# Hourglass attention and a MoE layer: both heads of a pair side by side in batch 0's AV output, transposed and up-sampled together

## Chip, cores, metric

One core of a Trainium2 chip. The metric is the device time of one execution in microseconds (us), the median of several runs. Engines: TensorE (PE, its weight loads PEld), VectorE (DVE), ScalarE (ACT), GpSimd (POOL), SyncE (SP).

## What is computed

Two layers, one after the other. The attention has two branches: one in which each query sees the keys within three positions, and one over sequences that are averaged by four, whose result is repeated four times. Their sum, tokens by 512, goes through a layer with a gated activation.

```python
# q, k, v: (8 batches, 8 heads, 576 tokens, 64)
q_d = q.reshape(B, H, Sd, 4, D).mean(axis=3)        # k_d, v_d alike; Sd = 144
out_up = np.repeat(sm_attn(q_d, k_d, v_d), 4, axis=2)
mask = np.abs(pos[:, None] - pos[None, :]) < 4      # local branch
scores = np.where(mask, scale * np.matmul(q, kT), -1e9)
attn_out = out_up + np.matmul(softmax(scores), v)
x = attn_out.transpose(0, 2, 1, 3).reshape(4608, 512)
h = x @ w_in                                        # (512, 2048)
out = (h / (1 + exp(-1.702 * h))) @ w_out           # (2048, 512)
```

## The kernel before

Heads go in four pairs (`hp`), with 64 values a head, so that a pair fills 128 partitions. The result of the attention is kept transposed, in `xT[hp]`, 128 partitions by all tokens; the MoE layer reads it in 9 groups of 512 tokens (`mm1`: 16 column blocks of `w_in`, four matmuls each, a silu on ScalarE; `mm2`: 4 token blocks, 16 matmuls each against `w_out`). Group 0 needs only batch 0. The attention of batch g + 1 is laid as `steps` between the matmuls of group g (L881-887), so batch 0 alone stands before any matmul that could cover it. The order on every engine is the order in which the code issues (`manual_schedule`, L44); POOL and SP also issue the DMAs, in that order.

The local branch works on 5 chunks of 114 queries, each as two halves (`par`) of 60 queries against 64 keys. The steps of batch 0:

- Scores, exponentials, and the cast of v into `vb` by VectorE, chunk by chunk as it lands (L777).
- `av_local` (L434): per chunk, half and head (`j`) a 64x64 matmul into one bank for each `par`; a head is put into partitions 0 to 63 or 64 to 127 by `pos`. Column 64 of each 65 is the sum of the weights. `warm` (L605) is a fp32 matmul of 512 columns on zeros that nobody reads; three of them stand between the parts (L795, L798).
- `prep_vd_pe` (L337): sums of four tokens of v, as 14 matmuls with the 0/1 matrix `psel` into `PA[2]`, then one ScalarE copy of 768 columns into `vd` (L352).
- `av_down` (L448): the averaged branch, 20 matmuls a head pair. Three blocks of 48 of its 144 queries come out in two columns (slots 5 and 6) of two banks.
- `normalise` (L470): a reciprocal of 14 sums and one product over 896 elements into `y`, on VectorE, per head pair; pair 3 uses the two banks `PM`, one at a time.
- `transp_sum` (L512): multiplies the averaged output with `up`, a 0/1 matrix that repeats each column four times (8 matmuls of 285 or 114 columns and 4 of 3 columns), and adds the 20 transposed 60x64 blocks of the local output in the same banks, by matmuls with an identity. Each matmul gives 64 partitions, so each is issued once for each head.
- `copy_x` (L553): four copies to `xT`, on ScalarE; for pair 3 the half `par` = 1 on VectorE.

The tail (L794-838) orders this and the first 24 matmuls of group 0: `turned` is `transp_sum` with `copy_x`; `part` issues matmuls of six accumulators `acc`, which lie in `PA` (three tiles of two banks), as soon as their `xT` is there. From column block 6 on, `late` says which bank `mm1` uses.

For batch 1, VectorE's transposes of q and k follow in its queue behind the last `copy_x`. The load of v for batch 1 (SP) waits for a VectorE copy behind those (L853), and on POOL the loads of the third and fourth quarter of `w_out` wait for that v (L855-859).

Of the kernel before, what the change touches and what calls it, by code (L numbers as in the profile page):

```python
# [8 lines left out]
FP32 = mybir.dt.float32  # L9
# [10 lines left out]
def kernel(  # L20
# [61 lines left out]
    UP = 5 + 240  # L82
# [30 lines left out]
    def iota_up():  # L113
        for par in range(2):
            for c in (0, 192):
                n = min(UP - c, 192)
                nc.gpsimd.iota(du[halves[par], c : c + n], pattern=[[1, n]],
                               base=-5 - 96 * par - (192 if c else 0) + c,
                               channel_multiplier=-1, **it)
# [217 lines left out]
    def prep_vd_pe(b, p, hp0=0, n=HP):  # L337
        vb, vd = vbs[b % 2], vds[b % 2]
        pv = p.rearrange("p x n -> p (x n)")
        for kc, iis in ((0, (0, 1)), (1, (1, 2, 3)), (2, (3, 4))):  # L340
            for i in iis:
                for j in range(2):
                    nc.tensor.matmul(  # L343
                        pv[64 * j : 64 * j + 64, 256 * kc : 256 * kc + D * n],
                        lhsT=psel[:, PSEL.index((i, kc)), :],
                        rhs=vb[:, i, :, :].rearrange(
                            "p (hp j) d -> p hp j d", j=2
                        )[:, hp0 : hp0 + n, j, 0:D],
                        start=(i == iis[0]), stop=(i == iis[-1]),
                        tile_position=(0, 64 * j),  # L350
                    )
        nc.scalar.copy(  # L352
            out=vd[:, :, hp0 : hp0 + n, 0:D],
            in_=pv[:, 0:768].rearrange("p (k h d) -> p k h d", k=3, h=HP)[:, :, 0:n],
        )
# [155 lines left out]

    def transp_sum(y, x):  # L512
        c0 = 20
        for par in range(2):
            edge = (0, 0) if par == 0 else (573, 285)
            for i0, ni, slot, t0 in ((0, 5, 5, 0), (2 - par, 2, 6, -192)):
                for j in range(2):
                    base = c0 + 384 * j + t0
                    nc.tensor.matmul(
                        sub(x[par][64 * j : 64 * j + 64], 57 * i0 + 3 * (1 - par),  # L520
                            (57, ni), (1, 57)),
                        lhsT=y[:, j, slot, :],
                        rhs=sub(up, base + 3 + 57 * par + 114 * i0, (114, ni), (1, 57)),
                        start=(slot == 5), stop=True,
                        tile_position=(0, 64 * j),
                        skip_group_check=True,
                    )
            for j in range(2):
                nc.tensor.matmul(
                    x[par][64 * j : 64 * j + 64, edge[1] : edge[1] + 3],  # L530
                    lhsT=y[:, j, 5, :],
                    rhs=sub(up, c0 + 384 * j + edge[0], (1, 3)),
                    start=False, stop=True,
                    tile_position=(0, 64 * j),
                    skip_group_check=True,
                )
        for i in range(5):
            for par in range(2):
                for j in range(2):
                    pos = j if par == 0 else 1 - j  # L540
                    c0 = 0 if (par == 1 or i == 0) else 3
                    c1 = 60 if (par == 0 or i == 4) else 57
                    nc.tensor.matmul(
                        x[par][64 * j : 64 * j + 64, 57 * i + c0 : 57 * i + c1],
                        lhsT=y[64 * pos : 64 * pos + 60, par, i, :],
                        rhs=ident(pos, 60, c0, c1),
                        start=False, stop=True,
                        tile_position=(64 * pos, 64 * j),
                        skip_group_check=True,
                    )  # L550
        return x

    def copy_x(b, hp, x):  # L553
        t0 = b * S
        for par in range(2):
            cp = nc.vector.tensor_copy if par and hp == HP - 1 else nc.scalar.copy
            cp(
                out=sub(xT[hp], t0 + 3 + 57 * par, (114, 5), (1, 57)),
                in_=sub(x[par], 3 - 3 * par, (57, 5), (1, 57)),
            )  # L560
            cp(
                out=sub(xT[hp], t0 + 573 * par, (1, 3)),
                in_=sub(x[par], 285 * par, (1, 3)),
            )
# [229 lines left out]
    for i0, i1 in ((0, 3), (3, 4)):  # L794
        warm(1)  # L795
        for hp in range(2):
            av_local(0, hp, o[hp], range(i0, i1))
    warm(1)  # L798
    prep_vd_pe(0, PA[2])
    make_mask()  # L800
    for hp in range(2):
        av_local(0, hp, o[hp], range(4, 5))
    for hp in range(2):
        av_down(0, hp, o[hp])
        y[hp] = normalise(o[hp])
    o[2] = av(0, 2, 2)
    y[2] = normalise(o[2])
    o[3] = PM
    av_local(0, 3, PM)
    av_down(0, 3, PM)  # L810
    y[3] = normalise(PM)

    gT0 = new_gT()
    acc = [PA[n][:, u, :] for n in range(3) for u in range(2)]
    late = PM + [acc[n] for n in (0, 2, 4)] + PM + [acc[1]] + PM
# [11 lines left out]
    turned(0, 0)  # L827
# [5 lines left out]
    turned(3, None)  # L833
# [84 lines left out]
```

## Time and profile before

| | us |
|---|---|
| median of 4 runs | 330.91 (329.95 to 332.26) |
| the profiled execution | 330.44 |
| its span, first to last instruction | 328.7 |
| TensorE busy in 0 to 19 us | 15.20 |
| TensorE busy in 19 to 31 us | 9.04 |
| TensorE busy in 31 to 43 us | 12.00 |
| TensorE busy in 43 to 66 us | 20.91 |
| TensorE busy in 66 to 180 us | 112.42 |
| TensorE busy in 180 to 328.7 us | 144.65 |

The granted TensorE clock is 1.00 in each of these stretches. The mean busy share of the DMA engines is 0.7 or more in every slice of the page up to 90 us.

How to read the lines that follow. A group line gives the source line, the engine, the operation, what is written and read, shapes (partitions x elements), the count, and then busy time, mean ns and idle time. A timeline line gives start, duration, engine, source line, operation, and in brackets the idle time of the engine just before and what ended it; "issue" means that nothing the profile shows ended it. A line of the waits gives total, number of times and longest, all in us. A line of the chain gives shares of the span.

### The profile page before, as it was taken

The page shows a single profiled execution, that of the slowest core. Times are in us where ns is not written, and L with a number is a line of the kernel's source. Part 1 is how long each engine was busy: PE and PEld are TensorE (multiplying, and loading weights), DVE is VectorE, ACT ScalarE, POOL GpSimd, SP SyncE. Part 2 cuts the span into 40 slices and gives each one's busy share as a digit, 9 for nine tenths or more (in the row PEclk, how much of TensorE's full clock was granted, in tenths as well). Part 3 has the DMA queues.
Part 4 walks back from the last instruction along what each step waited for, and adds up shares of the span by engine and source line. Part 5 has one row for each costly group of instructions (what it writes and reads, how often), then busy time and mean ns, then how long its engine had stood idle before and what let it go on. Part 6 is the DMA issues. An engine that isn't in the chain of part 4 may idle for free.

```text
span 328.7 us, 11237 instructions
## 1 busy us (share of the span) xinstructions
PE 314.2 (96%) x5024; PEld 157.5 (48%) x5024; DVE 131.1 (40%) x218; ACT 185.2 (56%) x325; POOL 138.0 (42%) x169
## 2 busy tenths in 40 slices
PE   6888999799899999999999999999999999999996
PEld 3444454444454555445544544445445544444444
DVE  6646342670568036803681267316730570000000
ACT  4633882465926583668366745675566647415711
POOL 7882860069504970398029800991098000000000
PEclk9999999999999999999999999999999999999999
DMA  7999989999715992499239931995190110011012
GB/s 127 181 201 210 184 132 197 169 203 248 166 38 135 187 186 78 122 198 187 76 102 199 197 88 66 189 196 133 40 173 2 56 46 32 2 65 63 0 55 75
DMA packets 63552, 41.10 MB, mean 125 GB/s; under 512 B 44048, under 2 KB 54416, under 8 KB 63504
## 3 DMA queue, kind: packets, MB, share of 16 engines
q1 hardware_dynamic: 52944, 26.42, 38.6%
q0 software_dynamic: 10416, 13.90, 25.0%
q8 instruction: 39, 0.64, 0.9%
q10 hardware_dynamic: 144, 0.07, 0.1%
q14 instruction: 9, 0.07, 0.1%
HBM read 44.83 MB, written 9.44 MB: 165 GB/s over the span
## 4 chain that ended last, share of the span: by engine, by line
PE 91%; DVE 4%; issue 3%; ACT 1%; POOL 1%; POOLq 0%; DVEq 0%; ACTq 0%
PE pm L650 35%; PE pm L706 35%; PE pa L379 4%; PE pa L650 3%; PE pa L440 2%; PE pa L398 2%; PE pm L608 2%; PE pa L493 2%; PE pa L462 2%; DVE y L479 1%; PE pa L706 1%; PE pm L721 1%; PE pa L343 1%; ACT vd L352 0%; DVE xT L590 0%
## 5 line engine op out<-in xcount | busy, mean ns | idle before, releaser
L706 PE MATMUL pm<-w_out_bf,gT 128*128 128x512 bf16 x528 | 121.8, 380 | 0.0
L650 PE MATMUL pm<-xT,w_in_bf 128*128 128x512 bf16 x536 | 118.7, 379 | 0.5 <-DVE xT L596 0.5
L661 ACT ACTIVATE gT<-pm 128x512 bf16<-128x512 f32 x134 | 79.9, 598 | 43.0 <-PE pm L650 43.0
L650 PEld LDWEIGHTS <-w_in_bf 128*128 128x128 bf16 x576 | 55.6, 98 | 67.3 <-issue 0.9
L706 PEld LDWEIGHTS <-gT 128*128 128x128 bf16 x560 | 51.6, 98 | 59.8 <-issue 0.6
L307 POOL TENSOR_TENSOR pq<-kT 128x576 f32<-128x576 bf16 x16 | 18.5, 1154 | 99.2 <-DVE kT L282 99.2
L423 DVE TENSOR_TENSOR es<-es,mask 128x600 bf16<-128x600 bf16 x28 | 21.5, 787 | 91.3 <-ACT es L409 90.6
L691 ACT ACTIVATE osb<-pm 128x512 f32<-128x512 f32 (+2 forms) x35 | 20.7, 593 | 40.6 <-PE pm L706 35.4
L569 ACT COPY od<-pa 128x384 f32<-128x384 f32 (+1 forms) x56 | 18.4, 411 | 32.2 <-DVE y L479 18.7
L479 DVE TENSOR_TENSOR y<-pa,rc 128x896 bf16<-128x896 f32 x31 | 33.8, 1091 | 1.1
L590 DVE TENSOR_TENSOR xT<-pa,od 128x570 bf16<-128x570 f32 x28 | 21.1, 753 | 11.8 <-ACT od L569 11.7
L328 POOL TENSOR_TENSOR v<-v 112x512 f32<-112x512 f32 x18 | 22.8, 1265 | 0.0
L693 DVE TENSOR_SCALAR osb<-pm 128x128 f32<-128x128 f32 x1 | 0.3, 291 | 55.3 <-ACT osb L691 55.3
L409 ACT ACTIVATE es<-pa 128x600 bf16<-128x600 f32 x32 | 19.7, 667 | 2.2 <-PE pa L379 1.9
L282 DVE STREAM_TRANSPOSE kT<-kb 128x576 f32<-128x576 f32 x16 | 20.0, 1249 | 0.7 <-DMA kb<-in_k_dram 0.4
L282 DVE STREAM_TRANSPOSE qT<-qb 128x576 f32<-128x576 f32 x16 | 19.8, 1237 | 1.1 <-DMA qb<-in_q_dram 1.1
L307 POOL TENSOR_TENSOR pq<-qT 128x576 f32<-128x576 bf16 x15 | 17.2, 1146 | 0.0
L478 DVE RECIPROCAL rc<-pa 128x14 f32<-128x14 f32 x31 | 7.5, 241 | 24.3 <-PE pa L462 24.3
L322 POOL CAST vb<-vf 128x2560 bf16<-128x2560 f32 (+1 forms) x9 | 16.0, 1798 | 0.0
L379 PEld LDWEIGHTS <-kT 32*64 32x64 bf16 x1280 | 12.1, 104 | 7.9 <-issue 6.5
L379 PE MATMUL pa<-qT,kT 32*64 32x60 bf16 x1280 | 14.0, 203 | 1.2 <-DVE qT L282 1.2
L331 POOL TENSOR_TENSOR vd<-v 112x256 bf16<-112x256 f32 x18 | 13.7, 759 | 1.4
(98 smaller groups left out, 256.0 us busy)
## 6 DMA issues: line engine op xcount, KB each, us to landing
vf<-in_v_dram SPq DMA_DIRECT2D x76, 128.0 KB, 6.2
out_dram<-osb SPq DMA_DIRECT2D x35, 256.0 KB, 2.1
v<-in_v_dram SPq DMA_DIRECT2D x36, 192.0 KB, 4.8
kb<-in_k_dram POOLq DMA_DIRECT2D x16, 288.0 KB, 7.3
qb<-in_q_dram POOLq DMA_DIRECT2D x16, 288.0 KB, 8.5
w_out_bf<-in_moe_w_out_dram POOLq DMA_DIRECT2D x4, 512.0 KB, 13.6
w_in_bf<-in_moe_w_in_dram POOLq DMA_DIRECT2D x2, 512.0 KB, 6.8
w_in_bf<-in_moe_w_in_dram POOLq DMA_DIRECT2D x1, 1024.0 KB, 12.5
```

The source lines that it names most:

```text
L282: nc.vector.transpose(out=t32.rearrange("p (i c) -> p c i", c=18), in_=store[b, qd].bitcast(FP32).rearrange("p (c d) -> p c d", c=18),)
L307: nc.gpsimd.tensor_tensor(out=t1, in0=sv[:, :, 0:2, :], in1=sv[:, :, 2:4, :], op=ALU.add)
L328: eng.tensor_tensor(out=t1[0:112], in0=x[:, :, 0:2, :], in1=x[:, :, 2:4, :], op=ALU.add)
L379: nc.tensor.matmul(sp[r // 2][64 * par : 64 * par + 64, r % 2, 60 * i : 60 * i + 60], lhsT=kT[b, qd][rows, k0 : k0 + 64, a], rhs=qT[b, qd] ...
L409: nc.scalar.activation(out=es[2 * qd + u][:, :, 0:300], in_=sp[u][:, :, 0:300], func=AF.Exp, scale=inv_sqrt_d,)
L423: nc.vector.tensor_tensor(out=ev, in0=ev, in1=mask, op=ALU.mult)
L479: nc.vector.tensor_tensor(out=y[:, xs], in0=ov[:, :, :, 0:D], in1=rc[:, xs].to_broadcast([128, n, 7, D]), op=ALU.mult,)
L590: eng.tensor_tensor(out=sub(xT[hp], t0 + 3, (57, 2), (114, 5), (1, 57)), in0=sub(x, 3, (509, 2), (57, 5), (1, 57)), in1=sub(od, 3, (57, 2) ...
L650: nc.tensor.matmul(acc, lhsT=w_in_bf[:, dmc, ffc * 128 : (ffc + 1) * 128], rhs=xT[dmc][:, g * TG : g * TG + TG], start=(dmc == 0), stop=(d ...
L661: nc.scalar.activation(out=gT[:, ffc, :], in_=acc, func=AF.Silu, scale=GELU_SCALE)
L691: eng.activation(out=osb, in_=ap, func=AF.Copy, scale=1.0 / GELU_SCALE)
L706: nc.tensor.matmul(ops[t], lhsT=gT[:, ffc, t * 128 : (t + 1) * 128], rhs=w_out_bf[:, ffc, :], start=(ffc == 0), stop=(ffc == n_ffc - 1),)
```

## The change

The changed kernel has `av_local0`, `av_down0` and `normalise0` for batch 0 alone; later batches keep `av_local`, `av_down`, `normalise` and `transp`.

- `av_local0` lets a chunk's parity choose the partition half (`pos`), and puts the two heads of a pair into columns side by side. A later transpose then reads 60 partitions by 128 columns, both heads at once: 10 matmuls instead of 20. `av_down0` puts its blocks into three slots, so that `transp_sum` repeats them for both heads with 5 matmuls instead of 12; `up` shrinks from 245 to 120 columns of four.
- `normalise0` writes two tiles, `yd` (256 elements, the averaged branch) and `yl` (768 elements, the local branch).
- `prep_vd_pe` takes a range of the three blocks: two first (10 matmuls, a copy of 512 columns), the third behind chunk 4's AV (4 matmuls, a copy of 256).
- Two `warm` calls instead of three between the parts of AV; `make_mask` (a ScalarE copy) later.
- `copy_x` makes three copies of 342, 228 and 6 columns instead of four; for pair 3 VectorE makes the last two.
- Bank order: pair 0 turns in `PM`; pair 3's AV goes to `PA[0]`, behind pair 0's turning; `acc` and `late` follow.

TensorE's program has 137 rows fewer, all before batch 1. The diff; of `transp_sum`, removed lines are left out:

```diff
@@ -79,7 +79,7 @@
         turn["m"] += 1
         return PM[turn["m"] % 2]
 
-    UP = 5 + 240
+    UP = 120
     wz = consts.tile([128, 512], FP32, name="wz")
     off = consts.tile([128, 60], BF16, name="off")
     psel = consts.tile([128, 7, 64], BF16, name="psel")
@@ -112,11 +112,8 @@
 
     def iota_up():
         for par in range(2):
-            for c in (0, 192):
-                n = min(UP - c, 192)
-                nc.gpsimd.iota(du[halves[par], c : c + n], pattern=[[1, n]],
-                               base=-5 - 96 * par - (192 if c else 0) + c,
-                               channel_multiplier=-1, **it)
+            nc.gpsimd.iota(du[halves[par]], pattern=[[1, UP]], base=-48 * par,
+                           channel_multiplier=-1, **it)
 
     def fill():
         nc.vector.memset(wz, 0.0)
@@ -334,10 +331,13 @@
             )
 
 
-    def prep_vd_pe(b, p, hp0=0, n=HP):
+    def prep_vd_pe(b, p, kcs=range(3)):
+        hp0, n = 0, HP
         vb, vd = vbs[b % 2], vds[b % 2]
         pv = p.rearrange("p x n -> p (x n)")
         for kc, iis in ((0, (0, 1)), (1, (1, 2, 3)), (2, (3, 4))):
+            if kc not in kcs:
+                continue
             for i in iis:
                 for j in range(2):
                     nc.tensor.matmul(
@@ -350,8 +350,10 @@
                         tile_position=(0, 64 * j),
                     )
         nc.scalar.copy(
-            out=vd[:, :, hp0 : hp0 + n, 0:D],
-            in_=pv[:, 0:768].rearrange("p (k h d) -> p k h d", k=3, h=HP)[:, :, 0:n],
+            out=vd[:, kcs[0] : kcs[-1] + 1, :, 0:D],
+            in_=pv[:, 256 * kcs[0] : 256 * kcs[-1] + 256].rearrange(
+                "p (k h d) -> p k h d", k=len(kcs), h=HP
+            ),
         )
 
 
@@ -509,59 +511,95 @@
                 )
         return x
 
+    def av_local0(hp, o, chunks):
+        E, vb = es[hp], vbs[0]
+        for i in chunks:
+            for j in range(2):
+                for par in range(2):
+                    pos, c0 = i % 2, 65 * (i // 2 * 2 + j)
+                    nc.tensor.matmul(
+                        o[64 * pos : 64 * pos + 64, par, c0 : c0 + 65],
+                        lhsT=E[64 * par : 64 * par + 64, j, 60 * i : 60 * i + 64],
+                        rhs=vb[64 * par : 64 * par + 64, i, 2 * hp + j, :],
+                        start=True, stop=True,
+                        tile_position=(64 * par, 64 * pos),
+                    )
+
+    def av_down0(hp, o):
+        Ed, vd, u = eds[hp // 2], vds[0], hp % 2
+        blocks = [(0, 3)] + [(kc, c) for kc in range(3) for c in (0, 1)]
+        blocks += [(kc, 2) for kc in range(3)]
+        for kc, c in blocks:
+            pos, slot = ((0, 6), (1, 6), (1, 4), (1, 5))[c]
+            for j in range(2):
+                q0 = SD * kc + 48 * c if c < 3 else 0
+                nc.tensor.matmul(
+                    o[64 * pos : 64 * pos + 64, j, 65 * slot : 65 * slot + 65],
+                    lhsT=Ed[64 * j : 64 * j + 48, u, q0 : q0 + 64],
+                    rhs=vd[64 * j : 64 * j + 48, kc, hp, :],
+                    start=(kc == 0), stop=(kc == 2 or c == 3),
+                    tile_position=(64 * j, 64 * pos),
+                )
+
+    def normalise0(o):
+        yl = work.tile([128, 2, 6, D], BF16, name="yl", tag="yl", bufs=4)
+        yd = work.tile([128, 2, 2, D], BF16, name="yd", tag="yd", bufs=4)
+        rc = work.tile([128, 2, 7, 1], FP32, name="rc", tag="rc")
+        ov = o[:, :, 0:455].rearrange("p x (c e) -> p x c e", e=65)
+        nc.vector.reciprocal(rc, ov[:, :, :, 64:65])
+        nc.vector.tensor_tensor(
+            out=yd.rearrange("p s x d -> p x s d"), in0=ov[:, :, 4:7:2, 0:D],
+            in1=rc[:, :, 4:7:2].to_broadcast([128, 2, 2, D]), op=ALU.mult,
+        )
+        nc.vector.tensor_tensor(
+            out=yl, in0=ov[:, :, 0:6, 0:D],
+            in1=rc[:, :, 0:6].to_broadcast([128, 2, 6, D]), op=ALU.mult,
+        )
+        return yl, yd
+
     def transp_sum(y, x):
...
+        y, yd = y
+        ups = [
+            (0, 6, sub(x[0], 3, (1, 228)), sub(up, 3, (228, 2), (1, 114))),
+            (0, 6, sub(x[0], 0, (1, 3)), sub(up, 0, (1, 3))),
+            (0, 4, sub(x[0], 231, (1, 117)), sub(up, 267, (1, 117))),
+            (1, 6, sub(x[1], 3, (1, 228)), sub(up, 117, (228, 2), (1, 114))),
+            (1, 4, sub(x[1], 156, (1, 75)), sub(up, 192, (1, 75))),
+        ]
+        for n, (bank, slot, to, what) in enumerate(ups):
+            nc.tensor.matmul(
+                to, lhsT=yd[:, slot // 2 - 2, :, :], rhs=what,
+                start=n in (0, 3), stop=True,
+                skip_group_check=True,
+            )
+        for i in range(5):
+            for par in range(2):
+                pos, m = i % 2, i // 2
+                c0 = 0 if (par == 1 or i == 0) else 3
+                c1 = 60 if (par == 0 or i == 4) else 57
+                a0 = 114 * m + 60 * par
                 nc.tensor.matmul(
...
+                    x[pos][:, a0 + c0 : a0 + c1],
+                    lhsT=y[64 * pos : 64 * pos + 60, par, 2 * m : 2 * m + 2, :],
+                    rhs=ident(pos, 60, c0, c1),
                     start=False, stop=True,
...
+                    tile_position=(64 * pos, 0),
                     skip_group_check=True,
                 )
...
         return x
 
     def copy_x(b, hp, x):
         t0 = b * S
-        for par in range(2):
-            cp = nc.vector.tensor_copy if par and hp == HP - 1 else nc.scalar.copy
-            cp(
-                out=sub(xT[hp], t0 + 3 + 57 * par, (114, 5), (1, 57)),
-                in_=sub(x[par], 3 - 3 * par, (57, 5), (1, 57)),
-            )
-            cp(
-                out=sub(xT[hp], t0 + 573 * par, (1, 3)),
-                in_=sub(x[par], 285 * par, (1, 3)),
-            )
+        other = nc.vector.tensor_copy if hp == HP - 1 else nc.scalar.copy
+        nc.scalar.copy(
+            out=sub(xT[hp], t0 + 3, (228, 3), (1, 114)), in_=sub(x[0], 3, (1, 342))
+        )
+        other(
+            out=sub(xT[hp], t0 + 117, (228, 2), (1, 114)), in_=sub(x[1], 3, (1, 228))
+        )
+        other(
+            out=sub(xT[hp], t0, (573, 2), (1, 3)), in_=sub(x[0], 0, (345, 2), (1, 3))
+        )
 
     def copy_od(x):
         od = work.tile([128, S], FP32, name="od", tag="od")
@@ -791,28 +829,28 @@
             func=AF.Exp, scale=inv_sqrt_d / 16.0,
         )
     nc.scalar.preload_act_table_set("silu_and_others")
-    for i0, i1 in ((0, 3), (3, 4)):
-        warm(1)
-        for hp in range(2):
-            av_local(0, hp, o[hp], range(i0, i1))
     warm(1)
-    prep_vd_pe(0, PA[2])
+    for hp in range(2):
+        av_local0(hp, o[hp], range(0, 2))
+    warm(1)
+    for hp in range(2):
+        av_local0(hp, o[hp], range(2, 4))
+    prep_vd_pe(0, PA[2], range(0, 2))
+    for hp in range(2):
+        av_local0(hp, o[hp], range(4, 5))
+    prep_vd_pe(0, PA[2], range(2, 3))
+    for hp in range(2):
+        av_down0(hp, o[hp])
+        y[hp] = normalise0(o[hp])
+    o[2] = PA[2]
+    av_local0(2, PA[2], range(5))
+    av_down0(2, PA[2])
+    y[2] = normalise0(o[2])
     make_mask()
-    for hp in range(2):
-        av_local(0, hp, o[hp], range(4, 5))
-    for hp in range(2):
-        av_down(0, hp, o[hp])
-        y[hp] = normalise(o[hp])
-    o[2] = av(0, 2, 2)
-    y[2] = normalise(o[2])
-    o[3] = PM
-    av_local(0, 3, PM)
-    av_down(0, 3, PM)
-    y[3] = normalise(PM)
 
     gT0 = new_gT()
-    acc = [PA[n][:, u, :] for n in range(3) for u in range(2)]
-    late = PM + [acc[n] for n in (0, 2, 4)] + PM + [acc[1]] + PM
+    acc = PM + [PA[n][:, u, :] for n in (1, 2, 0) for u in range(2)]
+    late = [acc[n] for n in (0, 1, 6, 2, 4, 0, 1, 7, 0, 1)]
 
     def part(ffcs, *dmcs):
         for dmc in dmcs:
@@ -824,13 +862,17 @@
         transp_sum(y[hp], x)
         copy_x(0, hp, x)
 
-    turned(0, 0)
+    turned(0, None)
+    o[3] = PA[0]
+    av_local0(3, PA[0], range(5))
+    av_down0(3, PA[0])
+    y[3] = normalise0(PA[0])
     turned(1, 1)
     part((0, 1), 0)
     turned(2, 2)
     part((0, 1), 1)
     part((2, 3), 0, 1)
-    turned(3, None)
+    turned(3, 0)
     part((0, 1, 2, 3), 2)
     part((4, 5), 0, 1, 2)
     part(range(6), 3)
```

## The prediction

> **What bounds it now.** The page's busy shares and its chain come first: they say which engine's time is the kernel's time.
>
> ```profile
> PE 314.2 (96%) x5024; PEld 157.5 (48%) x5024; DVE 131.1 (40%) x218; ACT 185.2 (56%) x325; POOL 138.0 (42%) x169
> PE 91%; DVE 4%; issue 3%; ACT 1%; POOL 1%; POOLq 0%; DVEq 0%; ACTq 0%
> ```
>
> TensorE is busy 314.2 of 328.7 us and is 91% of the chain. Only its idle time and its own small instructions can be won. The table of stretches puts 43 us of the span before 43 us, with 36.2 us busy, so the idle time is mostly in batch 0. The TensorE timeline of 19 to 31 us, where batch 0 turns the AV outputs into xT, shows where:
>
> ```profile
> 21.63 0.50 PE L462 MATMUL pa<-vd,ed 48*64 48x65 bf16 x36 [0.70 <-ACT vd L352]
> ...
> 23.53 0.37 PE L519 MATMUL pa<-up,y 128*64 128x285 bf16 x4 [0.63 <-DVE y L479]
> ...
> 24.81 0.37 PE L519 MATMUL pa<-up,y 128*64 128x285 bf16 x4 [0.42 <-DVE y L479]
> ...
> 27.70 0.24 PE L519 MATMUL pa<-up,y 128*64 128x114 bf16 x1 [1.20 <-issue]
> ...
> 30.56 3.63 PE L650 MATMUL pa<-xT,w_in_bf 128*128 128x512 bf16 x16
> ```
>
> Two waits are for a copy and for VectorE's normalisation. The 1.20 us is not a data wait: it stands in the middle of one head pair's up-sampling, and nothing releases it. From 30.56 us on TensorE doesn't pause until the next batch's AV. The waits of TensorE show the same "issue" later:
>
> ```profile
> PE pa L440 <- issue: 1.9, 2, 1.1
> PE pa L519 <- issue: 1.2, 1, 1.2
> PE pa L493 <- issue: 1.1, 1, 1.1
> PE pm L398 <- issue: 0.5, 1, 0.5
> ```
>
> They sit at 15.18, 27.70, 59.55, 90.67 and 192.01 us. In the order of TensorE's instructions these are numbers 429, 933, 1957, 2981 and 6565: 1,024, 1,024 and 3,584 apart, multiples of 256 (429 to 933 is 504, and the three fp32 `warm` calls between count as more than one instruction each). The DMA view has a queue for it:
>
> ```profile
> q8 instruction: 39, 0.64, 0.9%
> ```
>
> That is 16 KB a packet. Packets start at 25.47, 57.25, 88.06 and 188.82 us, and TensorE goes on 2.2 to 3.2 us after each start. So these are waits for the program itself, at every 256th instruction, when the packet was late. [...]
>
> **Batch 0, up to 31 us.** Sums against the profiled execution, 330.44 us for a span of 328.7.
>
> *Copy chain.* Now: three `warm` calls of 1.06 to 1.12 us between 16.08 and 19.75, 14 sums-of-four matmuls in 0.92 us (66 ns each), one copy of 0.80 us, then 20 AV matmuls; the first reciprocal starts at 22.11. Changed: one warm call fewer; AV of chunks 2 and 3 ends at about 18.6 (their casts end at 17.16), ten sums matmuls to 19.3. Copy cost on ScalarE from the rows 285 columns 0.40 and 768 columns 0.80: 0.165 + 0.82 ns a column, so 512 columns 0.59 and 256 columns 0.38. The changed program makes the last four sums matmuls wait for the first copy (one tile), so the two don't overlap: 19.35 + 0.59, four matmuls to 20.3, second copy to 20.75, the last 10 AV matmuls and drain 0.35. First reciprocal at 21.15: 0.95 earlier, of 1.1 for the warm call alone. The split itself thus wins nothing.
>
> *VectorE.* Rows: 896 elements 1.09 us, 448 elements 0.62, so 0.15 + 1.05 ns each. Now a head pair costs 0.28 + 1.01 = 1.27 us. Changed: 256 elements 0.42 and 768 elements 0.96 instead of 896, spaced 0.28 + 0.34 + 0.88 = 1.50. The four `yl` end at 22.7, 24.2, 25.7 and 27.2. For pairs 1 to 3 the up-sampling waits for the whole of `yl` all the same, because it writes the tile that `yl` reads; only pair 0 starts early.
>
> *Transposes.* Now 32 matmuls take 0.79 us a pair (24.81 to 25.60). Changed: 5 over 651 columns (0.216 us for 512 gives 0.28) and 10 transposes. No row shows 128-wide weights with 60 columns. Lower end: 14 ns now with four array quarters in turn, so 28 ns with two halves: 0.28 + 0.28 = 0.56. [...]
>
> *Sum.* Pair 2 starts at 25.77, ends 26.67; six matmuls of 0.216 to 27.97; pair 3 to 28.87, where 30.56 stands now: **-1.7 us** (-1.1 with 1.2, -2.4 with 0.56). Most of it is that block boundary 933 no longer falls in pair 2: it falls on the fourth matmul after pair 3, which is reached about 29.5, while its packet is usable about 27.1, if it comes as long after boundary 680 as now (5.5 us).
>
> *At no cost.* The shorter iota and exponentials for `up` end before 9.4 us, where ScalarE waits for scores anyway. The mask copy, 0.70 us, moves behind the second copy; the mask is first used at 45.47. `copy_x` is 0.45 + 0.3 + 0.17 instead of four copies, under six or ten matmuls (1.3 to 2.2 us). The bank order: the first late accumulator waits for the first silu (0.60), with five matmuls (1.08) between. No DMA moves: VectorE's four transposes for batch 1 wait for loads landing at 29.68 to 34.24, so the gate for v, and POOL's w_out loads behind it at 44.35, stay. That caps the gain: the third quarter of w_out is issued at 44.35, lands at 50.22, and its first matmul stands at 52.16 now. Up to there at most 1.9 us can be won.
>
> **Batches 1 to 7: where the blocks fall.** Nothing else changes; each is 1,201 to 1,205 rows. A packet starts 1 to 4 us after its block is entered and must precede the next boundary by 2.2 to 3.2.
> - Batch 1: boundary 1192 falls into the first scores, at about 41.6, and the next at the end of the second scores, 3.9 us later. DMA engines are full until 44, so the packet comes at about 43.6 and is usable near 46.2; needed at 45.5. **+0.7** (0 to +1.5).
> - The wait at 59.55 goes: its boundary falls in the second AV, 6.6 us after the one before. **-1.1**.
> - A boundary in the second scores followed by one in the first AV is what stalls at 90.67 and 192.01 (batches 2 and 5, 1.12 + 0.76): only 9 long matmuls (1.9 us) lie between. Counted out in the changed program, that pair falls in batches 3, 4, 6 and 7 instead, and in 2 and 5 no more. Three at 0.9 and batch 7, with hardly any transfers, at 0.3: +3.0 - 1.9 = **+1.1** (-0.5 to +2).
>
> Sum: -1.7 + 0.7 - 1.1 + 1.1 = **-1.0 us**: 329.4 against the profiled 330.44. The median, 330.91, lies 0.47 above that execution, so 329.9.
>
> **Rivals.**
> - *The fetches hide* (0.34). For: in batch 6 a boundary pair just beyond the AV costs nothing now, so the margin is tenths of a us. Against: both pairs of the stalling kind did stall. Then -1.7, no 0.7, -1.1 and -1.9: 330.9 - 4.7 = 326.2; half of it, 328.
> - *The gain is eaten* (0.15). [...]
> - *The array slows down* (0.08), the one that ends slower. [...]
> - That it doesn't do what it says is out: the program has 137 rows fewer on TensorE.
>
> **The numbers.** The sum's own case (0.43) gives 329.9, within 329.3 to 330.7. A measurement here can tell about 0.5% (1.65 us) from no change. Faster than 329.26: the hiding rival and the sum's lower edge, 0.37. Within: 0.55. Slower than 332.56: 0.08. Range 327.2 to 331.9: it leaves out the far end of the first rival (about 0.12) and the last (0.08).
>
> **What would show it.** Right: first reciprocal near 21.2; VectorE spacing 1.5; last up-sampling of pair 3 near 28.9; no issue wait at 27 to 28, 59 or 90; issue waits of about 1 us in the first AV of batches 3, 4 and 6. Wrong: issue waits elsewhere or none, a wait for w_out near 50, 15 matmuls of a pair in under 0.5 us, or a granted clock under 1.

## The result, and the profile after

The changed kernel takes 329.65 us (median of 43 runs, 327.26 to 333.32) against 330.91 (64 runs): ratio 0.9956, 95% interval 0.9943 to 0.9969, which is 1.0 to 1.9 us less. The forecast was 329.9. Ratios in this document leave out runs more than 1.5% above the fastest of their kernel; medians are of all runs.

The profiled execution took 327.26 us, with a span of 325.5; it is the fastest of its kernel, so the 3.2 us between the two profiles overstate the change. First the page's busy times, its chain and the queue of the program's packets:

```profile
PE 313.3 (96%) x4954; PEld 157.1 (48%) x4954; DVE 132.1 (41%) x220; ACT 185.2 (57%) x322; POOL 138.0 (42%) x167
...
q8 instruction: 38, 0.62, 0.8%
...
PE 89%; DVE 6%; issue 2%; ACT 1%; POOL 1%; ACTq 0%; POOLq 0%; DVEq 0%
```

TensorE has 70 matmuls fewer (4954 for 5024) and 0.9 us less busy time. The timeline of TensorE in batch 0 and at batch 1's second scores (L570 and L581 are the up-sampling and the transposes, L520 and L536 AV, L343 the sums of four):

```profile
15.53 1.13 PE L646 MATMUL pm<-wz 128*128 128x512 f32 x2 [0.58 <-ACT ed L827]
...
19.59 0.42 PE L343 MATMUL pa<-vb,psel 128*64 128x256 bf16 x4 [0.43 <-ACT vd L352]
...
20.47 0.45 PE L536 MATMUL pa<-vd,ed 48*64 48x65 bf16 x24 [0.25 <-ACT vd L352]
...
23.99 0.47 PE L570 MATMUL pa<-up,yd 128*128 128x228 bf16 x5 [0.65 <-DVE yl L554]
...
25.47 0.47 PE L570 MATMUL pa<-up,yd 128*128 128x228 bf16 x5 [0.20 <-DVE yl L554]
...
27.44 0.47 PE L570 MATMUL pa<-up,yd 128*128 128x228 bf16 x5
27.85 0.33 PE L581 MATMUL pa<-id,yl 60*128 60x60 bf16 x10
28.11 0.61 PE L688 MATMUL pm<-xT,w_in_bf 128*128 128x512 bf16 x2
...
45.91 0.28 PE L400 MATMUL pa<-qdT,kdT 32*64 32x144 bf16 x5 [0.78 <-issue]
```

The kernel before had there:

```profile
15.18 0.32 PE L398 MATMUL pm<-qdT,kdT 32*64 32x144 bf16 x7 [0.53 <-issue]
16.08 1.12 PE L608 MATMUL pm<-wz 128*128 128x512 f32 x2 [0.58 <-ACT ed L789]
```

From the first warm call to the start of the matmul behind pair 3 ("the end of pair 3" below) it was 16.08 to 30.56, 14.48 us, of which TensorE was busy for 11.52; now it is 15.53 to 28.11, 12.58 us, busy for 10.40. So of the 1.90 us won here 1.12 are work that is gone, of which the warm call is the largest piece, and 0.78 are idle time. No "issue" is left in pair 2; its up-sampling waits 0.20 us for VectorE. The 0.55 us ahead of the warm call is the wait of 0.53 us at boundary 429, which this execution did not have; profiles of kernels whose code is the same up to there do have it (e4 0.34 us, e7 0.66). The waits of TensorE for its program:

```profile
PE pa L442 <- issue: 0.8, 1, 0.8
PE pa L400 <- issue: 0.8, 1, 0.8
...
PE pa L464 <- issue: 0.2, 1, 0.2
```

They stand at 60.50, 45.91 and 155.56 us. Those of 59.55, 90.67 and 192.01 us before are gone: 1.8 us behind 31 us instead of 2.9.

The trace's records of the program's packets, set beside the instructions, give for each boundary when the block ahead of it was entered, when the packet started, and when TensorE went on (us):

| kernel | boundary in | block ahead entered | packet starts | TensorE goes on | issue wait |
|---|---|---|---|---|---|
| before | pair 2's up-sampling | 22.19 | 25.47 | 27.70 | 1.20 |
| before | batch 1's second AV | 54.57 | 57.25 | 59.55 | 1.06 |
| after | matmuls behind pair 3 | 21.01 | 24.43 | 28.77 | none |
| after | batch 1's second scores | 41.05 | 43.24 | 45.91 | 0.78 |
| after | batch 1's second AV | 54.13 | 57.90 | 60.50 | 0.82 |

Wherever TensorE waited, it went on 2.2 to 2.7 us behind the packet's start in these rows; in the row without a wait it arrived 4.3 us behind it.

### The profile page after: what moved, and what is told of

The parts are those of the page before. It is cut to its first block, busy times and chain, and to the rows that moved or that the text cites. A ratio compares the mean times of both kernels' runs of the same rounds, so it can differ in the third digit from the quotient of the medians.

```text
span 325.5 us, 11088 instructions
## 1 busy us (share of the span) xinstructions
PE 313.3 (96%) x4954; PEld 157.1 (48%) x4954; DVE 132.1 (41%) x220; ACT 185.2 (57%) x322; POOL 138.0 (42%) x167
## 4 chain that ended last, share of the span: by engine, by line
PE 89%; DVE 6%; issue 2%; ACT 1%; POOL 1%; ACTq 0%; POOLq 0%; DVEq 0%
PE pm L688 36%; PE pm L744 34%; PE pa L381 4%; PE pa L688 2%; PE pa L400 2%; PE pa L442 2%; PE pa L744 2%; PE pa L464 2%; PE pm L646 2%; PE pa L495 2%; DVE xT L628 1%; PE pm L759 1%; DVE y L481 1%; DVE yl L554 1%; PE pa L343 1%
## 5 line engine op out<-in xcount | busy, mean ns | idle before, releaser
L688 PE MATMUL pm<-xT,w_in_bf 128*128 128x512 bf16 x544 | 121.5, 379 | 0.9 <-DVE xT L634 0.9
L699 ACT ACTIVATE gT<-pm 128x512 bf16<-128x512 f32 x136 | 81.0, 598 | 45.7 <-PE pm L688 45.7
L481 DVE TENSOR_TENSOR y<-pa,rc 128x896 bf16<-128x896 f32 x28 | 30.6, 1091 | 1.0
L381 PEld LDWEIGHTS <-kT 32*64 32x64 bf16 x1280 | 12.1, 104 | 7.8 <-issue 6.1
L381 PE MATMUL pa<-qT,kT 32*64 32x60 bf16 x1280 | 14.0, 203 | 1.1 <-DVE qT L279 1.1
L480 DVE RECIPROCAL rc<-pa 128x14 f32<-128x14 f32 x28 | 6.7, 241 | 18.6 <-PE pa L464 18.6
```

What stands on the lines that cost most here:

```text
L381: nc.tensor.matmul(sp[r // 2][64 * par : 64 * par + 64, r % 2, 60 * i : 60 * i + 60], lhsT=kT[b, qd][rows, k0 : k0 + 64, a], rhs=qT[b, qd] ...
L481: nc.vector.tensor_tensor(out=y[:, xs], in0=ov[:, :, :, 0:D], in1=rc[:, xs].to_broadcast([128, n, 7, D]), op=ALU.mult,)
L688: nc.tensor.matmul(acc, lhsT=w_in_bf[:, dmc, ffc * 128 : (ffc + 1) * 128], rhs=xT[dmc][:, g * TG : g * TG + TG], start=(dmc == 0), stop=(d ...
L699: nc.scalar.activation(out=gT[:, ffc, :], in_=acc, func=AF.Silu, scale=GELU_SCALE)
```

## The experiments

The theory that went in: what decides is where every 256th instruction falls, and what of that is in batch 0's small matmuls. The rival: the side-by-side outputs and the shorter chain make the gain, wherever the blocks fall. Each ratio is to the kernel before on the same chip (medians there: 331.14 for e1 to e4, 331.03 for e5 to e8, 331.37 for e9 to e11, 330.77 for e12).

**e1, e2: the boundaries of batches 1 to 7 moved.** Tiny matmuls behind the first `mm1` shift them, in the kernel after to where they were before (70 matmuls), in the kernel before to where they are after (58).

```diff
         mm1(g, gT, steps, 0 if g else 6)
+        if g == 0:
+            for n in range(70):
+                r, c = n % 2, n // 2 % 2
+                nc.tensor.matmul(PA[1][64 * c : 64 * c + 64, r, 0:60],
+                    lhsT=id128[64 * r : 64 * r + 60, 0:64], ...)
```

> The changed kernel with 70 small identity matmuls (60x64 weights, 60 columns, in turn over four quarters of the array, into a free bank, read by nobody) at the end of the first MoE half of group 0: 140 rows of TensorE's program, so that from batch 1 on every 256th instruction falls on the same work as in the kernel before. Cost of the pad by the row of such matmuls: 70 x 14 ns = 1.0 us. Theory (block boundaries decide): the issue waits of the kernel before come back, 1.06 us in batch 1's transposes, 1.12 in batch 2's AV, 0.76 in batch 5's AV, and those of the changed kernel (0.78 and 0.8 us in batch 1, 0.2 in batch 4) go: about +0.6 us against the kernel before (-1.5 + 1.0 + 1.1). Rival (place doesn't matter): -0.5 us against the kernel before, and issue waits where the changed kernel has them.

> The kernel before with 58 such matmuls at the same place: 116 rows, so that from batch 1 on the boundaries fall where the changed kernel has them. Pad: 58 x 14 ns = 0.8 us. Theory: issue waits in the second scores and second AV of batch 1 (0.8 us each), none in batch 1's transposes nor in the AV of batches 2 and 5: -0.3 us against the kernel before. Rival: +0.8 us, issue waits where the kernel before has them.

e1: 331.98 us, 1.0019 (0.9998 to 1.0039), as the theory said. e2: 336.70 us, 1.0102 (1.0059 to 1.0145), far from both; one of its ten runs was at full clock (here: a mean of 0.9985 or more), with 332.4 us. The waits for the program in e1:

```profile
PE pa L442 <- issue: 1.0, 2, 0.6
PE pm L400 <- issue: 0.6, 1, 0.6
PE pm L744 <- issue: 0.2, 1, 0.2
PE pa L495 <- issue: 0.2, 1, 0.2
```

and in e2:

```profile
PE pa L398 <- issue: 2.2, 1, 2.2
PE pa L519 <- issue: 1.7, 1, 1.7
PE pa L379 <- issue: 1.3, 1, 1.3
PE pa L462 <- issue: 0.4, 2, 0.2
PE pm L398 <- issue: 0.3, 1, 0.3
```

e1's stand at 59.36, 90.07 and 191.18 us, as before. e2's stand at 47.15 and 53.44 us, in batch 1's first and second scores: one in the second scores was expected, with 0.8 us as in the kernel after, and has 2.2; the one in the first scores was not, and the one expected in the second AV isn't there. The added matmuls stand right ahead of the scores and leave the packet less time, which may be the reason; e5, with the matmuls elsewhere, was to tell.

**e3, e4: the third warm call alone.** Taken out of the kernel before, put back into the kernel after.

```diff
-    warm(1)
     prep_vd_pe(0, PA[2])
```

> The kernel before without the third of the three warm calls before the sums of four. Theory (the warm call is most of the gain in the copy chain, and the array keeps its clock): first reciprocal 1.1 us after its place less, and as the boundary in pair 2's up-sampling stays, pair 2 still waits for its packet, which starts the same time after the block before: 0.5 to 1.1 us of gain at the end of pair 3, so -0.8 us. Rival (clock): the granted clock falls under 1 in 19 to 31 us and the time is the same or longer.

> The changed kernel with the third warm call back, ahead of the sums of four. Theory: +1.1 us in the copy chain, all of it at the end of pair 3 (VectorE sets the pace there): -0.4 us against the kernel before. Rival (clock): the changed kernel loses clock in part of its executions by the missing warm call, and this one doesn't: mean clock 1.00 and the time is no longer than the changed kernel's, -1.5 us.

e3: 330.70 us, 0.9999 (0.9972 to 1.0025). e4: 329.82 us, 0.9961 (0.9943 to 0.9979), as the kernel after. Both expectations missed. In e3 the first reciprocal came at 20.77 us instead of 22.11 (5.0 us behind the first warm call instead of 6.0), but TensorE's timeline shows what became of it:

```profile
27.63 0.19 PE L529 MATMUL pa<-up,y 128*64 128x3 bf16 x1 [2.47 <-issue]
```

The packet started at 25.34 us (25.47 before), so the wait in pair 2 grew from 1.20 to 2.47 us, and pair 3 ended at 30.43 (30.56 before). Before the change, a shorter chain is worth nothing: the program's packet is what ends last. In e4 the call does delay the first reciprocal (6.4 us behind the first warm call instead of 5.4), and the time hardly shows it: among runs at full clock 329.2 us (8) against 329.0 in the kernel after. Its profile has some 7 us at half clock, so where the 1.06 us went is not shown.

**e5, e6: the same crossing, with the tiny matmuls early,** in a wait of 1.23 us ahead of batch 0's first scores, so that nothing stands right ahead of batch 1's.

```diff
+    for n in range(58):              # 70 in the kernel after
+        nc.tensor.matmul(PM[r][64 * c : 64 * c + 64, 0:16], ...)
     sp = scores(0, 0, barred=True)
```

> The kernel before with 58 tiny matmuls ahead of batch 0's first scores, where TensorE waits 1.23 us for its operands, so that every later block boundary of TensorE's program lies in batches 1 to 7 where it lies in the kernel after, and the one of pair 2 moves into pair 0's transposes (about 24 us). Theory (the places of the boundaries make most of the gain): the issue waits at 27.7, 59.6, 90.7 and 192 us vanish, one of 0.5 to 1.5 comes at 24, about 0.8 each come near 46 and 61: 329.9 to 330.6, ratio 0.996 to 0.998. Rival (the side-by-side outputs themselves make the gain): the waits change places without a sum, 331.1, ratio 1.000.

> The kernel after with 70 tiny matmuls ahead of batch 0's first scores: in batches 1 to 7 the boundaries lie where they lie in the kernel before, and in batch 0 one lies in pair 3's AV. Theory: issue waits return at about 59, 90 and 191 us (2 to 3 us in all), those near 46 and 61 go, one of 0.5 to 1.5 comes in pair 3's AV near 24 us: 331.0 to 332.0, ratio 1.000 to 1.003. Rival: as the kernel after, 329.8, ratio 0.996.

e5: 336.40 us, 1.0115 (1.0057 to 1.0172), missed by both. e6: 331.62 us, 1.0011 (0.9990 to 1.0032), as the theory said. In e5's timeline (its profile has a mean clock of 0.968, so only places are read from it) a boundary now lies in batch 0's second scores:

```profile
14.64 0.49 PE L379 MATMUL pa<-qT,kT 32*64 32x60 bf16 x39 [1.54 <-issue]
...
30.78 0.16 PE L529 MATMUL pa<-up,y 128*64 128x3 bf16 x1 [1.28 <-issue]
```

So e5 moved one boundary more than it was meant to. e6's waits, 1.5 us at 66.13 (L505) and 0.7 at 192.90 (L442), are at the kernel before's boundaries; of those expected near 59, 90 and 191 only the last came:

```profile
PE pa L505 <- issue: 1.5, 1, 1.5
...
PE pa L381 <- issue: 0.9, 1, 0.9
...
PE pa L442 <- issue: 0.7, 1, 0.7
...
PE pa L536 <- issue: 0.5, 1, 0.5
```

e1 and e6 together: with the boundaries of batches 1 to 7 where they were, the changed code gains nothing. But their profiles don't show that these boundaries are the cause. The first warm call and the end of pair 3, in e1 and then in e6:

```profile
16.07 1.13 PE L646 MATMUL pm<-wz 128*128 128x512 f32 x2 [0.58 <-ACT ed L827]
...
30.56 0.60 PE L688 MATMUL pm<-xT,w_in_bf 128*128 128x512 bf16 x2
...
16.90 1.13 PE L646 MATMUL pm<-wz 128*128 128x512 f32 x2 [0.62 <-ACT ed L837]
...
31.75 0.61 PE L688 MATMUL pm<-xT,w_in_bf 128*128 128x512 bf16 x2
```

Against the kernel after's profile (us):

| | to the first warm call | from there to the end of pair 3 | behind it |
|---|---|---|---|
| e1 | +0.54 | +1.91 | +0.12 |
| e6 | +1.37 | +2.27 | +0.67 |

Most of either loss lies in batch 0. Between the warm call and pair 3 e1 has the kernel after's own code; what differs is 6.8 us at half clock. e6 has its waits at L381 (0.9 us) and L536 (0.5) in the first two parts, and as much half clock. Behind pair 3 e1's waits are 1.3 us where the kernel after has 1.8, and its added matmuls take 0.7. Over all runs the clock lost 0.87% (e1) and 1.07% (e6), against 0.61% in the kernel after. At full clock e1 has four runs, with a median of 330.7 us, and e6 one, 329.1; the kernel after has 329.0. So the times of e1 and e6 are as the theory said, and what made them is not shown.

**e7, e8: the split copy of the sums of four.** e7 makes one copy of 768 columns again; e8 keeps two, with the third block in a bank of `PM`.

```diff
-    prep_vd_pe(0, PA[2], range(2, 3))
+    prep_vd_pe(0, PM[0], range(2, 3), 512)   # e8
```

> The kernel after with the sums of four of batch 0 copied once, 768 columns, as in the kernel before. Theory (the split wins nothing, since the last four sums wait for the first copy): first reciprocal within 0.15 us of 20.90, time within 0.2 us of the kernel after, ratio 0.996. Rival (the split wins 0.4 us of ScalarE's copy on the path): first reciprocal at 21.3 and ratio 0.997.

> The kernel after with the third block of the sums of four in a bank of PM instead of PA, so that its four matmuls don't wait for the first copy. Theory: the wait of 0.43 us for that copy goes, ScalarE makes the second copy right behind the first, the first reciprocal comes 0.2 to 0.4 us earlier; VectorE's chain passes it on to pairs 1 to 3: 0.2 to 0.4 us faster than the kernel after, ratio 0.995. Rival (the second wait, 0.25 us for the second copy, grows by as much): same as the kernel after, ratio 0.996.

e7: 329.31 us, 0.9953 (0.9936 to 0.9969). e8: 329.12 us, 0.9950 (0.9931 to 0.9969). Both are the kernel after within their intervals. Counted from the first warm call, the first reciprocal comes at 5.4 us in the kernel after, 5.0 in e7 and 4.9 in e8: the split as it was made costs 0.35 us of chain, since its second part waits for the first copy, and e8 mends that. e8's expected 0.2 to 0.4 us can't be told from nothing.

**The granted clock.** e8's profile gives the clue that the other kernels share. A table of stretches of 1 us (PEclk is the third number from the end; the DMA share behind it counts a packet's whole time where the packet starts, and so can pass 1):

```profile
core 0: us, PE busy (x) PEld busy (x) DVE busy (x) ACT busy (x) POOL busy (x), PEclk, DMA share, GB/s
22.00:23.00 1.00, 0.62 (x49) 0.56 (x42) 1.00 (x2) 0.80 (x3) 1.00 (x1) 1.00 1.15 213
23.00:24.00 1.00, 0.73 (x9) 0.45 (x10) 0.96 (x4) 0.07 (x1) 1.00 (x2) 0.62 1.13 219
24.00:25.00 1.00, 1.00 (x13) 0.54 (x13) 0.97 (x3) 0.56 (x2) 0.38 (x1) 0.50 1.10 207
25.00:26.00 1.00, 1.00 (x12) 0.55 (x12) 1.00 (x2) 0.31 (x2) 0.00 (x0) 0.50 1.09 205
26.00:27.00 1.00, 1.00 (x13) 0.52 (x11) 0.17 (x1) 0.62 (x2) 0.00 (x0) 0.68 1.15 217
27.00:28.00 1.00, 1.00 (x9) 0.54 (x7) 0.00 (x0) 0.25 (x2) 0.00 (x0) 1.00 1.10 208
```

Between 23 and 27 us the clock is 0.50: 0.38 + 0.50 + 0.50 + 0.32 = 1.70 us lost, so 3.4 us at half, from 23.24 us on. e5's profile has three such stretches:

```profile
core 0: us, PE busy (x) PEld busy (x) DVE busy (x) ACT busy (x) POOL busy (x), PEclk, DMA share, GB/s
16.00:17.00 1.00, 1.00 (x25) 0.67 (x24) 0.54 (x1) 0.41 (x1) 1.00 (x3) 0.55 0.71 89
...
26.00:27.00 1.00, 0.37 (x10) 0.23 (x9) 0.00 (x0) 0.84 (x2) 0.00 (x0) 0.83 1.12 211
...
29.00:30.00 1.00, 0.50 (x11) 0.37 (x12) 0.96 (x2) 0.00 (x0) 0.00 (x0) 0.87 1.09 203
...
36.00:37.00 1.00, 1.00 (x4) 0.29 (x2) 0.00 (x0) 0.00 (x0) 0.00 (x0) 0.71 1.23 205
...
57.00:58.00 1.00, 0.93 (x18) 0.61 (x18) 0.00 (x0) 0.08 (x1) 0.00 (x0) 0.53 1.11 203
...
60.00:61.00 1.00, 1.00 (x5) 0.35 (x4) 0.00 (x0) 0.11 (x1) 0.00 (x0) 0.77 1.14 215
```

Between these rows it is 0.50 up to 26, from 30 to 36 and from 58 to 60 us, and 1.00 elsewhere from 4 to 70 us. So they begin at 16.10 (17 - 2 x 0.45), 29.74 and 57.06 us and last 10.2, 6.8 and 3.4 us: their starts lie 13.64 and 40.96 us apart, 4 and 12 times 3.41. In other profiles they begin elsewhere, at 22.86 us in e1 and at 24.18 in e4. TensorE need not be without work ahead of one: in the 3.41 us ahead of e8's stretch TensorE was busy for 2.15 us, 63%, and in e1, e4 and e6 for 61 to 67%. Nor is such a share enough: in the profile of the kernel before two stretches of 3.41 us, from 21.38 and 24.79 us, were busy for 2.13 and 2.18 us, 62 and 64%, and the clock stayed at 1.00. What decides is open.

A mean clock of 0.995 is one such stretch, since 1.7 of 326 us is 0.5%, and 0.99 is two: e2's and e3's profiles have 3.4 us at half and a mean of 0.995, those of e1, e4 and e6 have 6.8 us, between 22 and 31 us, and a mean of 0.99. And most runs of both kernels have it: at 0.9985 or more were 42 of 150 runs of the kernel before (those beside the experiments, without one of 530 us at a clock of 0.56) and 13 of 44 of the kernel after; two stretches or more had 17 of 150 and 16 of 44; the mean loss is 0.46% and 0.61%. Among runs at full clock the medians are 330.3 and 329.0, so the gain isn't made of clock. The kernel after even loses 0.15% more, 0.5 us of clock. That costs less than 0.5 us of time: in e1's batch 0, 6.8 us at half clock, 3.4 us lost, cost 1.91 us, and a line through the runs gives 0.55 us of time (kernel after) to 0.65 us (before) for each us of clock lost. By that it gives back about 0.3 us.

**e9: e5 without its early wait.** The 58 matmuls behind the boundary at 15.2 us, in the wait for the exponentials.

```diff
     nc.scalar.preload_act_table_set("silu_and_others")
+    for n in range(58): ...          # into PA[2], 16 columns each
     for i0, i1 in ((0, 3), (3, 4)):
```

> As e5, the kernel before with 58 tiny matmuls, but behind the boundary at 15.2 us, in the wait of 0.58 us for the exponentials, so that the first scores of batch 0 keep their boundary where it was. Theory (a late program packet stops TensorE wherever the boundary stands in batch 0's small matmuls, and e5's extra loss came from its wait of 1.54 us and the half clock behind it): no wait of 1.5 us at 14.6, clock 0.99 to 1; the boundary in pair 0's up-sampling costs 1.0 to 2.0 us where pair 2 cost 1.2, nothing in pair 2: 330.5 to 331.8, ratio 0.998 to 1.002. Rival (the kernel before, whatever its boundaries, loses 3 to 5 us with these positions in batches 1 to 7): 334 to 336, ratio 1.010.

1.0032 (1.0008 to 1.0057), just above the theory's range, with a median of all 22 runs of 333.97: nine took 337.5 to 340.9 us at a mean clock of 0.980 or less. No wait at 14.6, none in pair 2, but one in pair 0, 3.46 us where 1.0 to 2.0 were expected:

```profile
23.66 0.17 PE L529 MATMUL pa<-up,y 128*64 128x3 bf16 x1
27.29 0.16 PE L529 MATMUL pa<-up,y 128*64 128x3 bf16 x1 [3.46 <-issue]
```

The block ahead was entered at 21.38, the packet started at 24.94 and TensorE went on at 27.29. TensorE was there at 23.83, 2.7 us earlier than it reached pair 2's boundary before (26.50); the packet came only 0.5 us earlier than that one (25.47). And during the wait the clock halves:

```profile
core 0: us, PE busy (x) PEld busy (x) DVE busy (x) ACT busy (x) POOL busy (x), PEclk, DMA share, GB/s
22.00:24.00 2.00, 1.20 (x80) 0.96 (x67) 1.93 (x4) 0.00 (x0) 1.74 (x2) 1.00 1.13 212
24.00:26.00 2.00, 0.00 (x0) 0.00 (x0) 1.93 (x5) 0.00 (x0) 2.00 (x2) 0.69 1.13 216
26.00:28.00 2.00, 0.71 (x23) 0.54 (x24) 1.26 (x3) 0.09 (x1) 0.31 (x1) 0.50 1.11 209
28.00:30.00 2.00, 2.00 (x34) 0.98 (x30) 0.00 (x0) 1.54 (x8) 0.32 (x1) 0.50 1.12 212
```

So the kernel before can't be had with the kernel after's boundaries at no price: with 70 matmuls more it has one boundary more in the stage. None of e2, e5 and e9 gave the kernel before any of the gain; e9's median is near the rival's 334 to 336, but its 13 runs at a clock of 0.985 or more have a median of 331.4, within the theory's 330.5 to 331.8, so that neither is settled.

**e10: dense matmuls in the waits.** On e8, four and six matmuls of 256 columns ahead of pairs 0 and 1.

```diff
+        fill_pe((4, 6, 0, 0)[hp])    # PM[1][:, 256:512] <- id128, psel
         transp_sum(y[hp], x)
```

> The kernel of e8 with ten matmuls of 256 columns and full 128-row weights (some 0.11 us each) that fill TensorE's waits for VectorE ahead of pairs 0 and 1 (0.27 and 0.65 us). Theory (half-clock stretches of about 3.4 us begin where TensorE is thinly used, at 20 to 24 us, and cost the kernels after some 0.6% of clock on average): fewer runs lose clock, mean loss under 0.2%, 328.5 to 329.0, ratio 0.993 to 0.994. Rival (the stretches come whatever these waits hold): loss as in e8, 0.3%, or as in the kernel after, 0.6%, and the fillers cost 0 to 0.4 us: 329.2 to 329.6, ratio 0.995 to 0.996.

327.50 us, 0.9885 (0.9851 to 0.9920): better than expected, and clear of the kernel after's interval. Five of six runs were at full clock (mean loss 0.18%). The fillers in TensorE's timeline:

```profile
21.10 0.61 PE L562 MATMUL pm<-psel,id 128*128 128x256 bf16 x4
21.55 0.47 PE L578 MATMUL pm<-up,yd 128*128 128x228 bf16 x5
...
23.42 0.82 PE L562 MATMUL pm<-psel,id 128*128 128x256 bf16 x6 [0.29 <-ACT xT L605]
24.07 0.47 PE L578 MATMUL pa<-up,yd 128*128 128x228 bf16 x5
```

Clock is only part of it: from 0.31% in e8 to 0.18% is at most 0.4 us, and the medians of the runs at full clock differ too, 328.8 (11 runs) and 327.3 (5). The ten matmuls also move every later boundary by 20 rows; the issue waits behind 31 us are 1.8 us in e10's profile and 3.3 in e8's. Which of the two gave more isn't settled.

**e11: batch 2's v held back,** until batch 1's first pairs are normalised.

```diff
-            loads_2()
...
                     st["y", hp] = normalise(st["o", hp])
+                if b == 1 and hps[0] == 0:
+                    load_v(2, gate=after(st["y", 1][0:1, 0, 0, 0:1], nc.vector))
+                    load_v4(2)
```

> The kernel after with the loads of v for batch 2 (float32 chunks and the sums-of-four source) held until batch 1's first pairs are normalised (about 57 us), so that fewer transfers are in flight from 48 to 57 us. Theory (program packets are late because they share the DMA engines with prefetches): the packet of 57.9 us starts 1 us earlier or more and the wait of 0.8 us at 60.5 is under 0.3: 0.3 to 0.8 us faster than the kernel after, ratio 0.993 to 0.995, unless batch 2 then waits for v. Rival (a packet starts at a fixed distance from its block's entry): wait unchanged, 329.6 to 330, ratio 0.996.

328.51 us, 0.9920 (0.9892 to 0.9948); it overlaps the kernel after's. The wait at 60 us fell to 0.25, as expected, but the packet came at 57.39, only 0.5 us earlier, and TensorE went on 2.28 us behind it instead of 2.60. The DMA share from 50 to 58 us is 1.15 and 1.09, hardly less than 1.14: the loads of q and k, which were not held back, may have filled it. So this doesn't tell whether prefetches make packets late.

**e12: e10 and e11 in one,** as the best version.

> The kernels of e10 and e11 in one: fillers in the waits ahead of pairs 0 and 1, and batch 2's v held until batch 1's first pairs are normalised. Theory (e10's gain is clock, e11's is earlier program packets and DMA room around 46 to 61 us; they add): nearly all runs at a clock of 0.998 or more, issue waits at 46 and 60 under 1.2 us together, 326.6 to 327.4, ratio 0.985 to 0.988. Rival (e11's gain was by chance the clock of its few runs): as e10, 327.5, ratio 0.9885, or later if batch 2 waits for v.

327.16 us, 0.9889 (0.9847 to 0.9930): as e10, as the rival said. Five of six runs were at full clock again, so 10 of 12 with the fillers, against 13 of 44 in the kernel after.

## Why the prediction was right, step by step

Its time, its sign and its main mechanism held: 1.0 us less was forecast and 1.5 (1.0 to 1.9) measured, the boundary left pair 2, and the gain is made in batch 0. Behind batch 0 two terms failed, and the sum came out near by luck. The terms:

- **Batch 0, -1.7.** Measured -1.90 from the first warm call to the end of pair 3, at full clock in both profiles (e11's, with the same code there, has 12.59 us too); in e1, at half clock for 6.8 us of it, the same code took 14.49. VectorE's spacing, 1.50, is 1.47 to 1.49.
- **Transposes and up-sampling of a pair, 0.9.** Mis-sized: 0.67 (27.44 to 28.11), 45 ns each over 15 matmuls, 0.12 less than the 0.79 before. The 0.9 in the sum (25.77 to 26.67), and the 1.2 beside it, were the author's estimates, and no run at full clock shows them: e7, e10, e11 and e12 have 0.66 or 0.67 for pair 3 too. The lower end, 0.56, was nearer.
- **Copy chain, 0.95 earlier, "of 1.1 for the warm call alone".** From the first warm call to the first reciprocal it was 6.0 us and is 5.4, so 0.7 (22.11 - 16.08 against 20.90 - 15.53). That the split wins nothing is right; it even costs 0.35 us of the chain (e7). But e3 shows that the earlier chain is worth nothing by itself: the sum counted it together with the boundary. The boundary's move without the shorter chain was not had by itself: e9 put it into pair 0, where it cost 3.46 us.
- **Batch 1's second scores, +0.7.** 0.78, at 45.91.
- **The wait at 59.55 goes, -1.1.** Failed. One of 0.82 us came at 60.50, a little further on in the same AV, and every profile with nearly these positions has it (e4 1.61, e7 0.77, e8 0.49). The step counted 6.6 us from one boundary to the next as enough; by the prediction's own bounds (packet up to 4 us behind the entry, 3.2 more to use) it wasn't. TensorE reached the next boundary 5.6 us behind the entry (at 59.68), and the packet, 3.8 us behind it, was usable only at 6.4.
- **Batches 3, 4, 6 and 7, three at 0.9 and one at 0.3.** Failed in size: 3.0 us was forecast, 0.18 measured, in batch 4. The three sibling profiles have 1.37, 0.52 and 1.60 us, in batch 4 every time, in batch 3 once (e4, 0.33) and in batch 6 once (e8, 0.53). So a pair of boundaries in those places is not enough. The kernel after's DMA share is a candidate: 0.19 from 124 to 128 us, around batch 3's first AV, and 0.57 from 152 to 156, ahead of batch 4's. No run tested it.
- **These errors cancel, by luck.** Behind 31 us the profiles at the kernel before's boundaries wait 2.94, 2.29, 1.32 and 2.36 us (before, e3, e1, e6), those at the kernel after's 1.78, 2.98, 2.11 and 3.34 (after, e4, e7, e8): means of 2.2 and 2.6, so +0.3 where the sum had +0.7. Within each group they differ by 1.6 us, so the 0.3 isn't clear of nothing.
- **The clock.** The rival that "the array slows down" (0.08) came in small form, one or two stretches of 3.4 us at half clock in most runs; the median, 329.65 us, stayed under its 332.56. Whether the missing warm call has a part in it isn't shown: with the call e4 has 0.45% of loss in the mean and the kernel before 0.46%; without it the kernel after has 0.61%, but e8 0.31%. The row "granted clock 1.00" of one execution did not stand for the runs: 108 of 150 of the kernel before had less.
- **The cap** of w_out's third quarter (landed at 50.41) was not reached: no wait for it.

In sum: -1.9 in batch 0, about +0.3 from later boundaries, about +0.3 from the clock: -1.3. Measured is -1.5 by the ratio and -1.3 between the medians; between the runs at full clock, where the last term has no part, it is -1.3 for -1.6. The traces show the first term; the other two are estimates, from a few profiles and from the spread of the runs.

## What to carry over

Removing instructions from a tuned stream, here 70 matmuls, also moves every later block of the program, so look for "issue" waits among small matmuls, take their distance in instructions, and count where they will stand afterwards: of the waits at 59.55, 90.67 and 192.01 us none is left, and three others came. What such a move is worth in time can't be read from one profile: e1's ratio lost the whole gain, and its profile shows shorter waits. A shorter chain is worth nothing while such a packet ends last (e3: the first reciprocal 1.34 us earlier, the end of pair 3 0.13), so ask which of the two is late before costing it. And read the clock of all runs, not of the one profile; ten dense matmuls put into waits of TensorE (e10) went with more further gain than the change itself, by clock, by moved boundaries or by both.

## What was not expected of the hardware

- A block of 256 instructions that was passed quickly, in 2.45 us, cost 3.46 us (e9). In the waits told here with the entry of the block ahead, the packet started 2.2 to 3.8 us after it (4.5 in e3), with a DMA share of 1.1 or more, and TensorE went on 2.2 to 2.7 us after that start (3.2 at 192.01 us before). Being there 2.7 us earlier brought the packet 0.5 us earlier (24.94 for 25.47). In e3, by the same count, the block was entered at 20.85, 1.3 us earlier than before, and the packet started at 25.34, only 0.1 us earlier.
- Half clock came in stretches of 3.4 us or multiples of it (3.4 in e8, 6.8 in e1, e4 and e6, 10.2 in e5), in e5 with starts 4 and 12 times 3.41 us apart, at other places in other profiles, in most runs of either kernel (108 of 150 and 31 of 44 below a mean of 0.9985), and in e8 with no wait of TensorE above 0.65 us in the 4 us ahead; the kernel before's profile passed two stretches of 3.41 us as thinly used (62 and 64% busy) at a clock of 1.00.
- In batch 0, where TensorE also waits, half clock cost less time than clock: 1.91 us for 3.4 us lost (e1).
